# Top-2 dispatch on one core: from every token through every expert to tiles of 256 gathered tokens, with the expert's weights addressed by a register

## The chip, the core and the metric

The kernel runs on one core of one Trainium2 chip. A core has five engines with queues of their own: TensorE (PE in the profile, with its weight loads listed as PEld), VectorE (DVE), ScalarE (ACT), GpSimd (POOL) and SyncE (SP). An engine takes its instructions in order; engines wait for each other, and for DMA transfers, through semaphores. The metric is the time on the device, in microseconds. The kernel before takes 1529.28 us, the median of three runs from 1528.74 to 1529.36 us.

## The reference, cut to what matters

Sixty-four heads of attention with a decay mask give x, and a layer of eight experts follows, of which each token uses its two best.

```python
scores = scale * np.matmul(q, k.transpose(0, 1, 3, 2))       # 8 batches, 8 heads, 576 x 64
ret = scores * Dmat                                          # gamma_h ** (i - j) for i >= j, else 0
x = np.matmul(ret, v)                                        # as (4608 tokens, 512)
noisy_logits = x @ w_gate + np.log1p(np.exp(x @ w_noise)) * noise
top2 = np.argpartition(-noisy_logits, 2, axis=1)[:, :2]      # 2 of 8 experts for each token
top2_w = softmax over the two
for e in range(8):
    for k in range(2):
        mask = top2[:, k] == e
        h = np.maximum(x[mask] @ w1[e], 0.0)                 # 512 -> 1024
        out[mask] += top2_w[mask, k, None] * (h @ w2[e])     # 1024 -> 512
```

## The kernel before

The program is written on a framework that orders the instructions of each engine by their priority and dependences when it is built, and puts in the waits. The order is fixed from then on.

**Attention** (L90 to L157). For each head and each pair of batches GpSimd issues twelve loads that cast to bf16 (L72, L75). TensorE transposes the queries and keys (L85), VectorE copies the result and multiplies it by the decay (L87, L106, L107). Then, for each batch and each block of 128 keys, TensorE makes the scores (L123), ScalarE copies them to SBUF (L126), GpSimd zeroes the part above the diagonal (L128) and TensorE multiplies by the values (L134, L139). ScalarE copies the result out (L153, L154), and SP writes it, transposed, to an HBM buffer xT (L156).

**Router** (L166 to L209). GpSimd reads xT back as bf16 into xTb, 512 tokens at a time (L176). For each of 36 tiles of 128 tokens there are eight matmuls of 8 columns (L183, L186), an exponential and a logarithm on ScalarE with the loads of their tables (L189 to L201), and nine small VectorE instructions that leave the weight of each of the eight experts, zero for six of them, in `gate` (L209).

**Experts** (L211 to L240). For each of the eight experts GpSimd loads the two weight matrices with a cast (L214, L215; two buffers of each). For each of nine groups of 512 tokens TensorE makes the hidden layer: 8 blocks of 128 hidden units with 4 matmuls each, the weights stationary and 512 tokens moving (L222); ScalarE applies the ReLU (L225). Then come 4 tiles of 128 tokens with 8 matmuls each, the hidden layer stationary and 512 columns of w2b moving (L230), and VectorE multiplies by the gate and adds into `out_acc`, which holds the whole output in SBUF (L234, L237). All tokens go through all experts: 8 x 9 x 64 = 4608 matmuls of 512 columns. Finally SP writes out_acc (L243).

## Time and profile before

| | |
|---|---|
| median of the runs | 1529.28 us |
| the profiled execution: span from the first to the last instruction | 1526.2 us |
| HBM read, written | 71.48 MB, 18.87 MB |
| TensorE's mean granted clock | 0.993 |
| matmuls issued: 1568 in attention and router, 4608 in the experts | 6176 |

The page of the profile gives no time of its own beside the span; the median of the runs is 3.1 us longer than the span. The span has three stages that follow each other almost without overlap: attention up to 416.6 us, reading xT back and the router up to about 540 us, and the experts. In the page's line of 40 slices each slice is 38.2 us long. Times of matmuls in the groups are from issue to the modelled end, so that they overlap; the rate is read from the chain of work or from the count in a window.

### The profile page before, as it was taken

How to read it: one execution, taken by the hardware profiler on the slowest of the kernel's cores; microseconds unless marked ns; L12 is line 12 of the kernel's file. 1: busy time of each engine (PE TensorE's matmuls, PEld its weight loads, DVE VectorE, ACT ScalarE, POOL GpSimd, SP SyncE). 2: the span in 40 equal slices, each digit the busy share in tenths (PEclk: the TensorE clock that was granted, in tenths of full speed). 3: DMA queues.
4: the chain of work that ended last, by engine and by line, in shares of the span. 5: the costliest groups of instructions: out<-in, count | busy, mean ns of one | idle time of the engine just before them, and what ended most of it. 6: DMA issues, size and time to landing. Idle time of an engine off the chain costs nothing.

```text
span 1526.2 us, 16572 instructions
## 1 busy us (share of the span) xinstructions
PE 1322.8 (87%) x6081; PEld 590.0 (39%) x6176; DVE 371.8 (24%) x1032; ACT 627.7 (41%) x1275; POOL 412.6 (27%) x738
## 2 busy tenths in 40 slices
PE   5777777777613599999999999999999999999998
PEld 2333333333201244444444444444444444444444
DVE  2222222222123332212221222122212221222122
ACT  4444444444479943333333333333333333333332
POOL 9999999999720000000000000000000000000000
PEclk9999999999999889999999999999999999999999
DMA  6666666665592000120030030020003003000122
GB/s 53 59 58 58 60 59 57 58 60 54 52 190 49 2 1 1 19 37 1 0 56 1 0 56 0 0 47 10 1 4 52 1 0 56 1 0 16 70 81 83
DMA packets 150657, 55.78 MB, mean 37 GB/s; under 512 B 124976, under 2 KB 137776, under 8 KB 150576
## 3 DMA queue, kind: packets, MB, share of 16 engines
q0 software_dynamic: 135088, 35.69, 23.6%
q1 hardware_dynamic: 15488, 19.03, 4.2%
q8 instruction: 48, 0.79, 0.2%
q14 instruction: 33, 0.27, 0.1%
HBM read 71.48 MB, written 18.87 MB: 59 GB/s over the span
## 4 chain that ended last, share of the span: by engine, by line
PE 74%; POOL 14%; ACT 7%; issue 2%; DVE 2%; DMA 0%; ACTq 0%; POOLq 0%
PE po L230 32%; PE phT L222 32%; POOL st L128 4%; PE pv_ps L134 4%; PE st_ps L123 3%; POOL q_bm L72 2%; POOL v_bm L72 2%; ACT L191 2%; PE tr_ps L85 2%; ACT L201 2%; POOL k_bm L72 2%; POOL q_bt L75 2%; POOL v_bt L75 2%; ACT st L126 1%; POOL k_bt L75 1%
## 5 line engine op out<-in xcount | busy, mean ns | idle before, releaser
L225 ACT ACTIVATE hT<-phT 128x512 bf16<-128x512 f32 x576 | 343.6, 597 | 638.1 <-PE phT L222 616.4
L222 PE MATMUL phT<-xTb,w1b 128*128 128x512 bf16 x2256 | 521.2, 384 | 5.1 <-ACT hT L225 2.1
L230 PE MATMUL po<-w2b,hT 128*128 128x512 bf16 x2257 | 511.1, 381 | 2.4
L237 DVE SCALAR_TENSOR_TENSOR out_acc<-po,gate,out_acc 128x512 f32<-128x512 f32 x252 | 189.2, 751 | 683.7 <-PE po L230 652.1
L222 PEld LDWEIGHTS <-w1b 128*128 128x128 bf16 x2304 | 224.8, 98 | 276.7 <-issue 18.4
L230 PEld LDWEIGHTS <-hT 128*128 128x128 bf16 x2304 | 225.6, 98 | 272.1 <-issue 3.6
L214 POOL DMA_DIRECT2D w1b<-in_moe_w_dram x8 | 6.0, 751 | 792.4 <-PE phT L222 789.2
L126 ACT ACTIVATE st<-st_ps 128x512 bf16<-128x512 f32 (+4 forms) x320 | 131.6, 425 | 190.5 <-PE st_ps L144 99.6
L123 PE MATMUL st_ps<-Qs,Ks 64*128 64x512 bf16 (+4 forms) x320 | 130.0, 436 | 46.2 <-DVE Ks L107 35.1
L128 POOL TENSOR_SCALAR_AFFINE_SELECT st<-st 128x512 bf16<-128x512 bf16 (+4 forms) x320 | 147.8, 510 | 19.7 <-ACT st L126 17.6
L134 PE MATMUL pv_ps<-st,v_bm 128*64 128x512 bf16 (+3 forms) x256 | 104.5, 454 | 18.7 <-POOL st L128 18.6
L87 DVE COPY qT<-tr_ps 128x128 bf16<-128x128 bf16 (+1 forms) x160 | 30.3, 215 | 214.1 <-PE tr_ps L85 214.1
L123 PEld LDWEIGHTS <-Ks 64*128 64x128 bf16 (+1 forms) x320 | 32.7, 113 | 115.7 <-issue 65.1
L186 PE MATMUL pn<-wn,xTb 128*128 128x8 bf16 x144 | 9.3, 169 | 53.7 <-ACT ns L189 53.7
L134 PEld LDWEIGHTS <-v_bm 128*64 128x64 bf16 x256 | 38.4, 150 | 40.4 <-issue 19.2
L72 POOL DMA_DIRECT2D q_bm<-in_q_dram x64 | 52.5, 820 | 0.0
L85 PE MATMUL tr_ps<-ident,k_bm 128*128 128x128 bf16 x128 | 25.1, 281 | 30.8 <-DMA k_bm<-in_k_dram 23.1
L72 POOL DMA_DIRECT2D k_bm<-in_k_dram x64 | 51.5, 805 | 0.0
L72 POOL DMA_DIRECT2D v_bm<-in_v_dram x64 | 50.4, 788 | 0.2 <-issue 0.2
L153 ACT ACTIVATE xs<-pv_ps 64x512 f32<-64x512 f32 x64 | 37.6, 587 | 27.3 <-ACT st L126 15.1
L234 DVE TENSOR_SCALAR out_acc<-po,gate 128x512 f32<-128x512 f32 x36 | 27.0, 750 | 83.5 <-PE po L230 83.5
L87 DVE COPY kT<-tr_ps 128x128 bf16<-128x128 bf16 (+1 forms) x160 | 29.0, 214 | 73.7 <-PE tr_ps L85 73.7
(55 smaller groups left out, 630.4 us busy)
## 6 DMA issues: line engine op xcount, KB each, us to landing
xT<-xs SPq DMA_DIRECT2D x64, 144.0 KB, 2.4
out_dram<-out_acc SPq DMA_DIRECT2D x36, 256.0 KB, 2.0
w1b<-in_moe_w_dram POOLq DMA_DIRECT2D x8, 1024.0 KB, 8.8
w2b<-in_moe_w_dram POOLq DMA_DIRECT2D x8, 1024.0 KB, 9.2
xTb<-xT POOLq DMA_DIRECT2D x9, 512.0 KB, 12.6
q_bm<-in_q_dram POOLq DMA_DIRECT2D x64, 64.0 KB, 2.6
k_bm<-in_k_dram POOLq DMA_DIRECT2D x64, 64.0 KB, 2.6
v_bm<-in_v_dram POOLq DMA_DIRECT2D x64, 64.0 KB, 2.7
```

What stands on the lines that cost most here:

```text
L72: nc.gpsimd.dma_start(out=bmain[:, :, bi * D:(bi + 1) * D], in_=src[:STS * P].rearrange("(t p) d -> p t d", p=P))
L75: nc.gpsimd.dma_start(out=btail[:, bi * D:(bi + 1) * D], in_=src[STS * P:])
L85: nc.tensor.matmul(pst[:, :kn], lhsT=src[:kn], rhs=ident[:kn, :kn], is_transpose=True, start=True, stop=True)
L87: nc.vector.tensor_copy(dst[:, j * P:j * P + kn], pst[:, :kn])
L123: nc.tensor.matmul(pst[:kn, :qlen], lhsT=Ksl[:, ko:ko + kn], rhs=Qsl[:, ko:ko + qlen], start=True, stop=True)
L126: nc.scalar.activation(st[:kn, :qlen], pst[:kn, :qlen], Act.Copy, scale=scale)
L128: nc.gpsimd.affine_select(st[:kn, :qlen], st[:kn, :qlen], pattern=[[1, qlen]], base=0, channel_multiplier=-1, compare_op=Alu.is_ge, fill=0.0)
L134: nc.tensor.matmul(po0[:, ko:ko + bn0], lhsT=vj, rhs=st[:kn, 0:bn0], start=(jb == 0), stop=(jb == STS - 1))
L222: nc.tensor.matmul(phT, lhsT=w1b[:, di, fi * P:(fi + 1) * P], rhs=xg[:, di, :], start=(di == 0), stop=(di == KD - 1))
L225: nc.scalar.activation(hT[:, fi, :], phT, Act.Relu)
L230: nc.tensor.matmul(po, lhsT=hT[:, fi, tsub * P:(tsub + 1) * P], rhs=w2b[:, fi, :], start=(fi == 0), stop=(fi == KF - 1))
L237: nc.vector.scalar_tensor_tensor(out_acc[:, t, :], in0=po, scalar=gate[:, t, e:e + 1], in1=out_acc[:, t, :], op0=Alu.mult, op1=Alu.add)
```

## The change

The router's result is used to send each token only to its two experts. The kernel has three functions now.

`attention` is as before, except that ScalarE writes its result as bf16 straight into an SBUF tile xT (L139, L140), and nothing is written to HBM and read back. Two of its pools have one buffer less: the raw inputs two instead of three, the decay vectors one instead of two. Its instructions have other line numbers: the loads L58 and L61, the transposes L71, the scores L109, the selects L114.

`dispatch` makes, for all 4608 tokens at once, the logits (L159), the best two experts (L178 to L199), and for each of the 9216 (token, expert) pairs a slot number in a list sorted by expert, by matmuls with a triangle of ones (L207, L209). Row numbers of tokens are put in the order of the slots by 72 rounds: for each column of 128 tokens and each of their two experts VectorE builds one-hot matrices of 384 and twice 128 columns (L269, L271, L273), and TensorE multiplies them (L277). Beside this each tile of 128 tokens is transposed back (L257), copied by ScalarE (L259), given four columns of its own (two weights, an expert, a slot; L260) and written as one row of 1040 bytes for each token to an HBM buffer xd (L261). Each expert's slots are filled up to a multiple of 256; the number of tiles of 256 slots is fixed at 43, the most that can be needed. `keep` holds for each tile its expert times 4096 (`eoff`) and the tokens' row numbers (`toki`).

`experts` goes through the 43 tiles. GpSimd gathers the tile's rows by two indirect DMAs of 128 rows (L353). TensorE transposes them (L384), loads the tile's offset into a register (L390) and makes the hidden layer with 32 matmuls of 256 columns whose stationary operand is addressed by the register (L399), and the output with 16 matmuls of 512 columns whose moving operand is (L414). The first step of tile i+1 is woven with the second of tile i, two to one. ScalarE and VectorE share the ReLU (L404, L406). ScalarE writes each tile's weighted output to y, which SP writes to an HBM buffer yd (L433, L434); a token's second visit gathers the row of its first (L426), VectorE adds it (L436), and an indirect DMA writes the sum to the token's row of the output (L438). Rows that are not wanted have a number out of bounds and are skipped. The weights of all eight experts, W1 and W2, are loaded once by 16 DMAs (L524, L527) and stay in SBUF.

```diff
+def dispatch(tc, K, xT, wgn, moe_noise, xd, keep):
...
+        for c in range(C):
+            pt = ps.tile([P, DM], BF16, name="pt", bufs=2)
             for di in range(KD):
+                nc.tensor.transpose(pt[:, di * P:(di + 1) * P], xT[:, di, c * P:(c + 1) * P], K["ident"])
+            xr = sp2.tile([P, XW // 2], F32, name="xr")
+            nc.scalar.activation(xr[:, :DM // 2].bitcast(BF16), pt, Act.Copy)
+            V.tensor_copy(xr[:, DM // 2:], pl[:, c, :])
+            nc.sync.dma_start(out=xd[c * P:(c + 1) * P, :], in_=xr)
...
+        for c in range(C):
+            for j in range(2):
+                ohi = sp2.tile([P, 3 * P], BF16, name="ohi")
+                V.tensor_scalar(ohi, K["iota"], hi[:, j, c:c + 1], None, Alu.is_equal)
+                olo = sp2.tile([P, 2, P], BF16, name="olo")
+                V.tensor_scalar(olo[:, 0, :], K["iota"][:, :P], lo[:, j, c:c + 1], K["pidx"][:, 0:1],
+                                Alu.is_equal, Alu.mult)
+                V.tensor_scalar(olo[:, 1, :], K["iota"][:, :P], lo[:, j, c:c + 1], float(c + 1),
+                                Alu.is_equal, Alu.mult)
...
+def experts(tc, K, W1, W2, keep, xd, yd, out):
...
+        def g1(i):
+            r = nc.tensor.value_load(keep["eoff"][0:1, i:i + 1], min_val=0, max_val=(E - 1) * KD * F)
...
+            for fp in range(KF // 2):
+                p1 = ps.tile([P, 2, TS], F32, name="p1", bufs=3)
+                for f2 in range(2):
+                    for di in range(KD):
+                        nc.tensor.matmul(p1[:, f2, :],
+                                         lhsT=W1[:, bass.ds(r + (di * F + (2 * fp + f2) * P), P)],
+                                         rhs=xgT[:, di, :], start=(di == 0), stop=(di == KD - 1))
+                        yield
...
+        def g2(i):
...
+            for fi in range(KF):
+                for s in range(2):
+                    nc.tensor.matmul(po[s], lhsT=hT[:, fi, s * P:(s + 1) * P],
+                                     rhs=W2[:, bass.ds(r + fi * DM, DM)],
+                                     start=(fi == 0), stop=(fi == KF - 1))
...
+            for s in range(2):
+                if i:
+                    nc.gpsimd.indirect_dma_start(
+                        out=pv[:, s, :], out_offset=None, in_=yd[:i * TS, :],
+                        in_offset=IOff(ap=st[i]["pi"][:, s:s + 1], axis=0),
+                        bounds_check=i * TS - 1, oob_is_err=False)
...
         for e in range(E):
-            w1b = wep.tile([P, KD, F], BF16)
-            w2b = wep.tile([P, KF, DD], BF16)
-            for g in range(NGRP):
...
-                for fi in range(KF):
-                    phT = mps.tile([P, GRP], F32, bufs=2)
...
-                        nc.tensor.matmul(phT, lhsT=w1b[:, di, fi * P:(fi + 1) * P],
...
-                        nc.tensor.matmul(po, lhsT=hT[:, fi, tsub * P:(tsub + 1) * P],
```

How the order moves, at the places of which the prediction speaks. First **TensorE in the middle of the experts**; phT and p are the hidden layer's PSUM tiles, W_65 and W_66 the two resident weight tiles, and an ISA row is an instruction of TensorE's sequencer that works out an address from the register. Before:

```order
L222 LDWEIGHTS w1b
L222 MATMUL phT<-xTb,w1b 128x512
L222 LDWEIGHTS w1b
L222 MATMUL phT<-xTb,w1b 128x512
L222 LDWEIGHTS w1b
```

The changed kernel, in the middle of a tile:

```order
L414 LDWEIGHTS hT
L414 ISA
L414 MATMUL po<-W_66,hT 128x512
L399 ISA
L399 LDWEIGHTS W_65
L399 ISA
L399 MATMUL p_10924<-xgT,W_65 128x256
L399 ISA
L399 LDWEIGHTS W_65
L399 ISA
L399 MATMUL p_10924<-xgT,W_65 128x256
```

Each matmul of 256 columns has become four instructions, two of them address arithmetic, and each matmul of 512 columns three. In the program each ISA row holds two or three arithmetic steps on registers: the offset in bytes is the register times two, to which a constant is added.

Second, **GpSimd in the experts**. Before, it only issues the weights of the experts to come:

```order
L214 DMA w1b<-in_moe_w_dram 128x4x1024
L215 DMA w2b<-in_moe_w_dram 128x8x512
L214 DMA w1b<-in_moe_w_dram 128x4x1024
L215 DMA w2b<-in_moe_w_dram 128x8x512
L214 DMA w1b<-in_moe_w_dram 128x4x1024
```

The changed kernel, one tile with its waits (DMASW is GpSimd's own DMAs, DMAHW those of SP; prv is the gathered row of the first visit, xg the gathered tile):

```order
L438 DMA out_dram<-o,oi 4608x512 [waits DMASW6_49,DMASW2_49,DVE_49]
L426 DMA prv_5846<-yd,pi 128x512 [waits DMAHW3_49,DMASW7_49]
L438 DMA out_dram<-o,oi 4608x512 [waits DMASW6_49,DVE_49]
L426 DMA prv_5846<-yd,pi 128x512 [waits DMASW1_49]
L353 DMA xg_5843<-xd,toki 128x260 [waits DVE_49,PE_49]
L353 DMA xg_5843<-xd,toki 128x260 [waits DMASW3_49,PE_49]
```

Six indirect DMAs belong to each tile. The two that write the output wait for VectorE, the first that reads yd waits for SP's write of the tile before, and the two that gather a tile wait for TensorE to have transposed an earlier one. The tile gathered here is seven ahead of the one whose old rows are gathered beside it.

Third, **VectorE in the dispatch**. Before, at the place of the router (nl, ev, msk, gv, gsum and gate are tiles of 8 columns or 1):

```order
L196 TENSOR_TENSOR nl<-nl,pg 128x8
L209 TENSOR_SCALAR gate<-gv,gsum 128x8
L198 MAX mx<-nl 128x8
L195 TENSOR_TENSOR nl<-ns,noise_t 128x8
L190 TENSOR_SCALAR ns<-ns 128x8
```

The changed kernel, in the middle of the 72 rounds (ohi and olo are the one-hot matrices):

```order
L269 TENSOR_SCALAR ohi<-iota_f,hi 128x384
L260 COPY xr<-pl 128x4
L271 TENSOR_SCALAR olo<-iota_f,lo,pidx 128x128
L273 TENSOR_SCALAR olo<-iota_f,lo 128x128
L260 COPY xr<-pl 128x4
L269 TENSOR_SCALAR ohi<-iota_f,hi 128x384
L271 TENSOR_SCALAR olo<-iota_f,lo,pidx 128x128
L273 TENSOR_SCALAR olo<-iota_f,lo 128x128
```

Nine small instructions for each of 36 tiles have gone, and three long ones for each of 72 rounds have come, with the 36 copies into the rows of xd between them.

More of the change, by code (lines that the diff above doesn't have):

```diff
@@ L11 @@
 BF16 = mybir.dt.bfloat16
+I32 = mybir.dt.int32
 AX = mybir.AxisListType.X
@@ L14, with attention @@
 Act = mybir.ActivationFunctionType
-@with_exitstack
-def kernel(
-    ctx: ExitStack,
-    tc: tile.TileContext,
-    q: bass.AP,
-    k: bass.AP,
-    v: bass.AP,
-    moe_w_gate: bass.AP,
-    moe_w_noise: bass.AP,
-    moe_noise: bass.AP,
-    moe_w1: bass.AP,
-    moe_w2: bass.AP,
-    out: bass.AP,
-):
+P = 128
+N = 4608
+NCOL = N // P
+E = 8
+F = 1024
+DM = 512
+KD = DM // P
+KF = F // P
+TS = 256
+NTILE = 43
+HPE = N // P
+NHI = E * HPE
+XW = DM + 8
+BIG = 1.0e6
+IOff = bass.IndirectOffsetOnAxis
+def attention(tc, q, k, v, xT):
     nc = tc.nc
     B, H, S, D = q.shape
-    N, DD = out.shape
-    E = moe_w_gate.shape[1]
-    F = moe_w1.shape[2]
-    assert (B, H, S, D) == (8, 8, 576, 64)
-    assert (N, DD, E, F) == (4608, 512, 8, 1024)
-    P = 128
-    NT = N // P
-    KD = DD // P
-    KF = F // P
-    GRP = 512
-    NGRP = N // GRP
     STS = 4
     STL = S - STS * P
-    dram = ctx.enter_context(tc.tile_pool(name="dram", bufs=1, space=bass.MemoryType.DRAM))
-    xT = dram.tile([P, KD, N], F32)
     scale = 1.0 / math.sqrt(D)
     with tc.tile_pool(name="attn_const", bufs=1) as consts, \
-         tc.tile_pool(name="attn_head", bufs=2) as headp, \
-         tc.tile_pool(name="attn_raw", bufs=3) as rawp, \
+         tc.tile_pool(name="attn_head", bufs=1) as headp, \
+         tc.tile_pool(name="attn_raw", bufs=2) as rawp, \
          tc.tile_pool(name="attn_qk", bufs=2) as qkp, \
          tc.tile_pool(name="attn_st", bufs=4) as stp, \
-         tc.tile_pool(name="attn_psum", bufs=2, space=bass.MemoryType.PSUM) as ps, \
-         tc.tile_pool(name="attn_out", bufs=3) as outp:
+         tc.tile_pool(name="attn_psum", bufs=2, space=bass.MemoryType.PSUM) as ps:
         ident = consts.tile([P, P], BF16)
```

400 lines of the change are left out of this document (324 added, 76 removed).

## The prediction

> **What bounds the kernel now.** I read the page first: its busy times and its line of 40 slices.
>
> ```profile
> span 1526.2 us, 16572 instructions
> ...
> PE 1322.8 (87%) x6081; PEld 590.0 (39%) x6176; DVE 371.8 (24%) x1032; ACT 627.7 (41%) x1275; POOL 412.6 (27%) x738
> ...
> PE   5777777777613599999999999999999999999998
> ```
>
> The slices show two kernels in one: up to slice 15 TensorE has gaps, from slice 16 on it is full. The shares over the whole span hide that, so I cut it at the ends of the stages (columns: length, busy time and count of each engine, granted clock, DMA share, GB/s).
>
> ```profile
> core 0: us, PE busy (x) PEld busy (x) DVE busy (x) ACT busy (x) POOL busy (x), PEclk, DMA share, GB/s
> 0.00:416.60 416.60, 302.92 (x1280) 126.54 (x1280) 116.93 (x384) 186.83 (x529) 391.47 (x711) 1.00 0.63 57
> 416.60:540.00 123.40, 42.20 (x359) 20.55 (x365) 38.96 (x353) 103.99 (x181) 11.35 (x15) 0.93 0.48 76
> 540.00:1523.00 983.00, 977.73 (x4444) 442.94 (x4532) 215.63 (x297) 336.92 (x565) 9.82 (x12) 1.00 0.11 23
> ```
>
> GpSimd bounds attention (391 of 417 us). The middle stage is mostly ScalarE (104 of 123 us). The experts are TensorE alone, at the full clock, and how fast is read from the chain in order of time:
>
> ```profile
> 552.67 6.91 PE phT L222 x32
> ...
> 587.29 6.91 PE po L230 x32
> ```
>
> 32 matmuls of 512 columns take 6.91 us: 0.216 us each, 0.42 ns per column. 4608 of them would be 995 us; some run before 540 us. This stage is 64% of the span, and three quarters of its work is multiplied by a gate of zero.
>
> **The change part by part.** I build the changed kernel's span stage by stage.
>
> *Attention* keeps its GpSimd instructions in the same order, with the first two weight loads pushed in near its end. With one raw buffer less, a pair's inputs are overwritten two pairs later; a pair takes 416.6/32 = 13.0 us, and its inputs are read within that. That cover hides the edit; without it each pair would wait about one landing (2.6 us, row below), 83 us in all. I take 416.6, with ScalarE's xT write in the place of the old one.
>
> *Dispatch* is a chain on VectorE, whose instructions I price by these rows (group: count, busy us, mean ns; two rows of the timeline: start, duration):
>
> ```profile
> L234 DVE TENSOR_SCALAR out_acc<-po,gate 128x512 f32<-128x512 f32 x36 | 27.0, 750 | 83.5 <-PE po L230 83.5
> L209 DVE TENSOR_SCALAR gate<-gv,gsum 128x8 f32<-128x8 f32 x36 | 8.1, 225 | 0.0
> L190 DVE TENSOR_SCALAR ns<-ns 128x8 f32<-128x8 f32 x36 | 5.8, 161 | 32.6 <-ACT ns L189 32.6
> L191 ACT ACT_TABLE_LOAD x31 | 39.8, 1283 | 0.5
> ...
> 433.01 0.23 DVE L200 TENSOR_SCALAR ev<-nl,mx 128x8 f32<-128x8 f32 x1
> ...
> 433.14 0.23 DVE L203 TENSOR_SCALAR msk<-nl,mx 128x8 f32<-128x8 f32 x1
> ```
>
> A VectorE instruction with a scalar from memory costs 0.225 us for 8 columns and 0.750 for 512, so 1.04 ns per column on top of about 0.22; with a constant the fixed part is 0.16. Independent ones start 0.13 us apart though they last 0.23, so 0.1 of the fixed part overlaps. One round of the 72 is then 0.62 + 0.35 + 0.35 - 0.27 = 1.05 us, together 76 us. The bounds: 53 us if SBUF operands stream at twice the rate (the 750 ns row reads PSUM), 95 us with no overlap. I take 76, since every row measured has the overlap, and 4 us for the 36 copies between. Around them: logits and their copy 6 us (288 short matmuls at most), two tables and two activations 3.5, fifteen instructions of 288 columns at 0.46 and eleven small ones 9, 36 dependent additions at 0.2 7, ranks 4, tail 5. Dispatch: 76 + 4 + 34.5 = 114.5 us, against 123.4 for the stage that it replaces. It ends at 531.
>
> Three things lie beside it. ScalarE's 36 copies of a token tile, at the 0.6 us that it needs for 512 columns (row below), are 22 us. The writes to xd hold up VectorE's copies only if four of them need longer than eight rounds (8.4 us). And the weights:
>
> ```profile
> L126 ACT ACTIVATE st<-st_ps 128x512 bf16<-128x512 f32 x64 | 38.2, 597 | 134.0 <-PE st_ps L144 99.6 <-PE pv_ps L139 22.7 <-PE st_ps L123 10.3
> ...
> 432.00:436.00 4.00, 0.60 (x12) 0.48 (x12) 0.67 (x5) 3.55 (x6) 1.22 (x2) 1.00 1.31 206
> ...
> q_bm<-in_q_dram POOLq DMA_DIRECT2D x64, 64.0 KB, 2.6
> out_dram<-out_acc SPq DMA_DIRECT2D x36, 256.0 KB, 2.0
> ```
>
> While weights and xTb load together the queues move 206 GB/s. Sixteen weights of 1.05 MB and the 4.8 MB of xd are 21.6 MB, 105 us: all has landed near 522. That is 9 us ahead of need, the thinnest cover in the plan.
>
> *Start of the experts*: two indirect issues at the 0.82 us of a GpSimd DMA, a landing of 2.6, transposes, and ScalarE's copy of 1024 columns (1.1): 6 us, so 537. *End*: two VectorE additions, two issues, a landing, the closing: 6 us.
>
> *A tile* decides. TensorE's streaming is 32 x 256 + 16 x 512 + 8 x 128 columns at 0.42 ns: 7.35 us. That alone would be 316 us for 43 tiles. But each tile now passes 80 address computations (ISA) through TensorE's sequencer, 32 weight loads and 48 matmuls that take their address from a register, and 32 plain instructions. Nothing in this trace computes an address on TensorE. The nearest rows are instructions that the sequencers handle themselves (min/median/max ns), and the router's short matmuls:
>
> ```profile
> L85 PEldq EVENT_SEMAPHORE  x128: 51/51/51, 6.0 to 406.4; - x128
> ...
> L258 POOLq MOVE  x1: 35/35/35, 0.1 to 0.1; - x1
> ...
> L258 ACTq EVENT_SEMAPHORE  x1: 17/17/17, 0.7 to 0.7; - x1
> ...
> 471.68 0.25 PE L186 MATMUL pn<-wn,xTb 128*128 128x8 bf16 x4 [5.80 <-ACT ns L189]
> ...
> L186 PE MATMUL pn<-wn,xTb x144: 165/168/215, 426.4 to 525.4; 128*128 128x8 bf16 x144
> ```
>
> Four pairs of weight load and matmul take 0.25 us, of which the last takes 0.168: a pair each 27 ns, 13.5 ns for a plain instruction. TensorE's own sequencer instruction, a semaphore wait, takes 51 ns, and a register move (GpSimd's) 35. So an ISA costs between 51 ns (the arithmetic free) and 51 + 3 x 35 = 156; I take the middle, 104. An instruction with a register address costs between 13.5 and 51 + 35 = 86; I take 51, the row of the same sequencer. Then 80 x 0.104 + 80 x 0.051 = 12.4 us, the plain ones 0.4, and 1.4 for the register load (between the 51 ns of a sequencer instruction and the 2.0 us of a DMA's landing) and the waits. **A tile takes 14.2 us**, and streaming hides beneath it: TensorE is bound by its sequencer. The bounds are 7.35 (80 x 0.0645 = 5.2 would vanish under streaming) and 80 x 0.242 + 2.8 = 22.2 us.
>
> [...]
>
> GpSimd's six DMAs per tile come next (group rows as above):
>
> ```profile
> L72 POOL DMA_DIRECT2D q_bm<-in_q_dram x64 | 52.5, 820 | 0.0
> L75 POOL DMA_DIRECT2D v_bt<-in_v_dram x64 | 36.1, 564 | 0.9 <-issue 0.9
> L215 POOL DMA_DIRECT2D w2b<-in_moe_w_dram x8 | 7.1, 885 | 41.3 <-PE po L230 30.8 <-PE phT L222 6.9 <-DMA xTb<-xT 3.6
> ```
>
> An issue costs 0.56 to 0.89 us; reading 128 row numbers may double it. Six are 3.4 to 10.7 us, and the second output write waits out the first's landing (2.0 less an issue). At 0.82 that is 6.1 us: hidden under 14.2. The first gather from yd waits for ScalarE's two copies (1.2) and SP's write (2.0 to 2.6) after the tile's last matmul, some 4.5 us, with the output writes and gathers of later tiles behind it on GpSimd; with five issues after it, it is through at 8.6, inside a tile of 14.2. Should the tile shrink below that, this wait is the next thing late. VectorE (two additions 1.5, two ReLUs 1.2, eleven small ones 2) and ScalarE (1.1 + 1.2 + 1.2) are under 5 us.
>
> **The sum.** 416.6 + 114.5 + 6 + 43 x 14.2 + 6 = 1154 us of span. The median of the runs lies 3.1 us above the profiled span, so **1157 us**.
>
> **The rivals.** *A: register addresses are nearly free.* Then streaming, or GpSimd at up to 10 us, bounds the tile: 7.35 to 10 us, 546 + 43 x 8.5 = 912 us, up to 976. For it speaks how close plain instructions follow each other; against it that TensorE's only sequencer instruction in the trace takes 51 ns where ScalarE's, the same, takes 17 (rows above). *B: slower.* If an instruction with a register address is not sent until the matmul ahead of it is done, nothing overlaps on TensorE any more. A matmul of 512 columns takes 379 ns from issue to end (row below), one of 256 about 275, a weight load 98. 32 x (0.208 + 0.098 + 0.275) + 16 x (0.104 + 0.098 + 0.379) = 28 us, and 546 + 43 x 28 = 1750 us. It decides from 22.9 us on: (1529.3 - 546)/43.
>
> ```profile
> L230 PEld LDWEIGHTS <-hT 128*128 128x128 bf16 x2304 | 225.6, 98 | 272.1 <-issue 3.6
> L222 PE MATMUL phT<-xTb,w1b x2256: 375/379/635, 482.8 to 1515.2; 128*128 128x512 bf16 x188
> ```
>
> For B speaks that no such instruction is in the trace, against it that streams of matmuls with waits overlap freely here.
>
> [...]
>
> *C: a late dispatch*: the weights or xd's writes starve the rounds (95 us for the rounds, 30 more for the writes): 1200 us. *D: it does not skip what it says*: 43 tiles run whether filled or not, 11008 slots for 9216 pairs; this is in the sum already and has no chance of its own.
>
> **How the numbers follow.** The forecast, a sequencer-bound tile of 10 to 20 us, has 0.65, with C inside it; A has 0.23, B 0.09, and 0.03 are left for tiles of 20 to 22.9 us. The forecast alone spans 976 to 1406. The range for eight in ten takes in most of A and stops where the upper bounds meet: 915 to 1400 us. A measurement of this kernel tells 0.2% from no change. Only B is slower: slower 0.09, faster 0.90, the same 0.01.
>
> **What would show it.** In the changed profile: the middle slices of TensorE well under nine tenths in the experts though nothing releases it late (idle before L399 put down to issue); 43 tiles evenly 14 us apart; ISA rows near 104 ns on TensorE's sequencer; GpSimd idle in each tile. A: TensorE at nine tenths, or GpSimd full, and tiles of 7 to 10 us. B: matmuls that start only at the end of the one before. Dispatch is right if L353's first start is near 531 us. The forecast is wrong if the tile is not bound by TensorE's sequencer.

## The result, and the profile after

The changed kernel takes 1022.4 us (median of four runs, 1019.43 to 1022.85), the kernel before 1529.0 us beside it (1528.37 to 1529.36). The ratio is 0.668, with a 95% interval of 0.667 to 0.669. The forecast was 1157 us: right in sign, inside its range, and 135 us too long. The profiled run took 1022.85 us, its span 1021.1 us. Of the kernels below, two have one execution that is over 1.5% longer than the fastest of its kernel (1033.6 us with the weights in the attention, 1100.4 us with six buffers), and their medians are given without it.

First the view of the changed kernel cut at the ends of its stages (columns as before: length, busy time and count of each engine, granted clock, DMA share, GB/s).

```profile
core 0: us, PE busy (x) PEld busy (x) DVE busy (x) ACT busy (x) POOL busy (x), PEclk, DMA share, GB/s
0.00:418.20 418.20, 303.01 (x1280) 126.08 (x1281) 120.56 (x387) 189.41 (x529) 396.60 (x724) 1.00 0.57 38
418.20:560.40 142.20, 58.84 (x513) 39.76 (x512) 86.54 (x365) 24.70 (x41) 15.18 (x20) 0.90 0.77 144
560.40:1001.50 441.10, 412.68 (x2408) 219.51 (x2408) 173.87 (x600) 149.02 (x214) 254.03 (x251) 0.98 0.38 120
1001.50:1021.10 19.60, 0.11 (x1) 0.00 (x0) 1.50 (x2) 1.04 (x2) 5.05 (x5) 0.50 0.17 54
```

Set against the terms of the sum (the first tile's matmuls start at 567.7 us, so 7.3 us of the third row are the start of the experts):

| Term | Predicted | Measured | Difference |
|---|---|---|---|
| Attention | 416.6 | 418.2 | +1.6 |
| Dispatch | 114.5 | 142.2 | +27.7 |
| Start of the experts | 6 | 7.3 | +1.3 |
| 43 tiles | 43 x 14.2 = 610.6 | 433.8 = 43 x 10.09 | -176.8 |
| End | 6 | 19.6 | +13.6 |
| Span | 1153.7 | 1021.1 | -132.6 |

So the tile decided, as the prediction said, and it came out 29% shorter. Two terms were too small. The rows on TensorE's sequencer (PEldq is what the sequencer does in the queue of weight loads; count: min/median/max ns, first and last start):

```profile
L399 PEldq FUSED_REGOPS  x2752: 37/46/51, 567.3 to 992.7; - x197
...
L414 PEldq FUSED_REGOPS  x688: 42/46/51, 574.6 to 1000.0; - x172
...
L390 PEldq TENSOR_LOAD <-eoff x14: 295/299/494, 555.9 to 566.1; - x14
...
L390 PEldq TENSOR_LOAD <-eoff x29: 297/300/451, 694.1 to 983.2; - x29
```

An address computation, which the order listed as ISA, is the row FUSED_REGOPS: two or three operations in one instruction, 46 ns where the prediction took 104 and set the floor at 51. The register load is 300 ns. The last two rows are of two windows: fourteen loads run before the first tile, twenty-nine later, one per tile.

The pace shows in the starts of the output's matmuls (L414), eight of them in 3.9 us:

```profile
L414 PE MATMUL po<-W,hT x8: 376/376/377, 744.8 to 748.7; 128*128 x8
```

Two matmuls of W1 and one of W2 form a group. A group takes 3.9/7 = 0.56 us here and 0.545 us in the median of the starts from 590 to 690 us, while its 1024 columns stream in 0.43. The group holds five address computations, five instructions with a register address and one plain weight load: if the sequencer works them off one after the other, (545 - 5 x 46 - 13.5)/5 = 60 ns are left for an instruction with a register address, where the prediction took 51. This is an estimate from these rows and from the prediction's 13.5 ns.

From the starts of every 32nd matmul at L399 a tile takes 8.9 to 9.2 us from the third to the thirteenth, 9.5 to 9.9 from the fourteenth to the twenty-second, mostly 10.0 to 10.6 after that, and 11.7 to 12.3 in the last three. What the other engines waited for in this time (engine, line, releaser: us in total, times, longest):

```profile
DVE oi L365 <- DMA out_dram<-o,oi: 115.3, 39, 5.5
DVE pi L375 <- DMA prv<-yd,pi: 64.0, 25, 4.4
PEld L399 <- issue: 55.6, 184, 2.4
...
DVE isA L359 <- DMA xg<-xd,toki: 49.5, 26, 5.2
```

VectorE stands for transfers that still read its small buffers (L365, L375), or have yet to fill a gathered tile (L359), and ReLUs and additions stand behind it. In the last tiles, where no gathers of xd are left, GpSimd shows a chain that repeats every 12 us: an output write, the wait for its landing, the second one, two gathers, their landing, VectorE's addition. VectorE's waits for the small buffers stand in the same chain, just ahead of the addition (two timelines, GpSimd and VectorE: start, duration, [idle before, releaser]).

```profile
954.51 1.01 POOL L438 DMA_INDIRECT out_dram<-o,oi  x1 [4.31 <-DVE o L436]
958.06 1.00 POOL L438 DMA_INDIRECT out_dram<-o,oi  x1 [2.55 <-issue]
959.36 1.04 POOL L426 DMA_INDIRECT prv<-yd,pi  x1 [0.30 <-issue]
960.71 1.02 POOL L426 DMA_INDIRECT prv<-yd,pi  x1 [0.30 <-issue]
966.61 1.01 POOL L438 DMA_INDIRECT out_dram<-o,oi  x1 [4.88 <-DVE o L436]
...
960.91 0.16 DVE L365 SCALAR_TENSOR_TENSOR oi<-isA,tokf 128x2 int32<-128x2 f32 x1 [4.24 <-DMA out_dram<-o,oi]
965.51 0.16 DVE L375 SCALAR_TENSOR_TENSOR pi<-isA,pf 128x2 int32<-128x2 f32 x1 [4.43 <-DMA prv<-yd,pi]
965.58 0.74 DVE L436 SCALAR_TENSOR_TENSOR o<-po,g,prv 128x512 f32<-128x512 f32 x1
```

In the dispatch one wait stands out, and a smaller one behind it:

```profile
DVE nl L165 <- DMA noise<-in_moe_noise_dram: 30.6, 1, 30.6
DVE xr L260 <- DMA xd<-xr: 16.1, 14, 3.5
```

The noise is issued at 417.75 us, when its buffer opens, and lands at 454.1, behind the weights. VectorE does nothing for 30.6 us of that time.

### The profile page after: what moved, and what is told of

Same layout as the page of the kernel before. It is cut to its first block, busy times and chain, and to the rows that moved or that the text cites. A ratio compares the mean times of both kernels' runs of the same rounds, so it can differ in the third digit from the quotient of the medians.

```text
span 1021.1 us, 16704 instructions
## 1 busy us (share of the span) xinstructions
PE 774.6 (76%) x4201; PEld 385.3 (38%) x4201; DVE 382.5 (37%) x1354; ACT 364.2 (36%) x785; POOL 670.9 (66%) x998
## 5 line engine op out<-in xcount | busy, mean ns | idle before, releaser
L399 PE MATMUL p<-xgT,W 128*128 128x256 bf16 x1376 | 325.0, 273 | 19.0 <-DVE hT L406 14.0
L414 PE MATMUL po<-W,hT 128*128 x688 | 259.7, 381 | 4.1 <-DVE hT L406 4.0
L399 PEld LDWEIGHTS <-W 128*128 x1376 | 132.6, 96 | 192.2 <-issue 55.6
L438 POOL DMA_INDIRECT out_dram<-o,oi x86 | 86.9, 1011 | 119.8 <-DVE o L436 52.1
L109 PE MATMUL st_ps<-Qs,Ks 64*128 64x512 bf16 (+4 forms) x320 | 129.7, 435 | 46.7 <-DVE Ks L93 35.1
L114 POOL TENSOR_SCALAR_AFFINE_SELECT st<-st 128x512 bf16<-128x512 bf16 (+4 forms) x320 | 148.1, 514 | 18.2 <-ACT st L112 16.6
L353 POOL DMA_INDIRECT xg<-xd,toki x86 | 86.4, 1005 | 84.6 <-DVE toki L330 39.6
L404 ACT ACTIVATE hT<-p 128x512 bf16<-128x512 f32 x86 | 51.4, 597 | 239.2 <-PE p L399 231.5
L426 POOL DMA_INDIRECT prv<-yd,pi x84 | 85.8, 1021 | 28.1 <-issue 25.7
L436 DVE SCALAR_TENSOR_TENSOR o<-po,g,prv 128x512 f32<-128x512 f32 x86 | 64.2, 746 | 37.8 <-DMA prv<-yd,pi 24.2
L109 PEld LDWEIGHTS <-Ks 64*128 64x128 bf16 (+1 forms) x320 | 32.6, 113 | 117.2 <-issue 67.2
L414 PEld LDWEIGHTS <-hT 128*128 128x128 bf16 x688 | 66.4, 97 | 21.2 <-DVE hT L406 4.4
L433 ACT ACTIVATE y<-po,g 128x512 f32<-128x512 f32 x86 | 54.8, 685 | 41.2 <-PE po L414 33.5
L386 ACT ACTIVATE xgT<-pt 128x1024 bf16<-128x1024 bf16 x43 | 44.0, 1024 | 55.2 <-DVE cm L370 48.4
L277 PE MATMUL pT<-olo,ohi 128*128 128x256 bf16 x216 | 42.6, 308 | 23.3 <-DVE olo L273 18.4
L406 DVE TENSOR_SCALAR hT<-p 128x512 bf16<-128x512 f32 x86 | 58.7, 682 | 0.0
L58 POOL DMA_DIRECT2D q_bm<-in_q_dram x64 | 52.6, 822 | 0.1
```

The source lines that it names most:

```text
L109: nc.tensor.matmul(pst[:kn, :qlen], lhsT=Ksl[:, ko:ko + kn], rhs=Qsl[:, ko:ko + qlen], start=True, stop=True)
L114: nc.gpsimd.affine_select(st[:kn, :qlen], st[:kn, :qlen], pattern=[[1, qlen]], base=0, channel_multiplier=-1, compare_op=Alu.is_ge, fill=0.0)
L353: nc.gpsimd.indirect_dma_start(out=xg[:, s, :], out_offset=None, in_=xd[:, :], in_offset=IOff(ap=keep["toki"][:, 2 * i + s:2 * i + s + 1], ...
L399: nc.tensor.matmul(p1[:, f2, :], lhsT=W1[:, bass.ds(r + (di * F + (2 * fp + f2) * P), P)], rhs=xgT[:, di, :], start=(di == 0), stop=(di == ...
L406: V.tensor_relu(hT[:, 2 * fp:2 * fp + 2, :], p1)
L414: nc.tensor.matmul(po[s], lhsT=hT[:, fi, s * P:(s + 1) * P], rhs=W2[:, bass.ds(r + fi * DM, DM)], start=(fi == 0), stop=(fi == KF - 1))
```

## The experiments

Two theories stood against each other. **S**: TensorE's sequencer sets the tile. **G**: GpSimd's and VectorE's order of transfers, landings and dependent work sets it, and the sequencer has room. For the dispatch: **N**, the wait for the noise is all on the path, against **W**, the weights' transfers hold the rest as well.

The kernel before takes 1529.0 to 1529.2 us whenever it runs. The changed kernel doesn't: 1022.4 us in its first runs, 1061.5 in its last (below). The experiments were made on three chips, and only on the last of them beside the changed kernel. So times are compared where they were made together, and where a stage is set against the first runs of the changed kernel, the text says so. On one chip the fixed experts, the twelve small buffers, the early noise and the longer arithmetic were run; on a second the pinned order with and without registers, the weights in the attention, and all of these; on the third six buffers with and without registers, the changed kernel again and the twelve small buffers again.

### Fixed experts

```diff
-  lhsT=W1[:, bass.ds(r + (di * F + (2 * fp + f2) * P), P)],
+  lhsT=W1[:, (i * E // NTILE) * KD * F + di * F + (2 * fp + f2) * P: ... + P],
```

and the same at W2.

> Left out of the computation: the choice of the expert. Each tile takes the weights of a fixed expert (the constant i*8//43), so the register arithmetic and the register-addressed loads and matmuls of the tiles are gone; tables, gathers, scatters and every other instruction stay. Theory S (TensorE's sequencer sets the tile: a group of two W1 matmuls and one W2 matmul takes 0.545 us for 0.43 us of streaming): the group falls to 0.43 us and the tile from 10.08 us to what comes next, GpSimd's six indirect transfers at 1.31 us from start to start, 7.9 us, with some waits 8.2; 43 x 1.9 = 81 us less, 941 us (920 to 965). Rival G (the tile is set by GpSimd's order of scatter, landing and gather, about 10 us, and the sequencer has room): the tile stays at 9.7 to 10.1 us, 1005 to 1022 us.

Measured: 1022.1 us (1018.9 to 1023.5). The time of theory S (941 us) didn't come, although the group fell to the 0.43 us that it had named. Theory G's time came (1005 to 1022 us), its even tiles of 9.7 to 10.1 us only in the mean. Four starts in 1.3 us:

```profile
L414 PE MATMUL po<-W,hT x4: 379/379/379, 820.3 to 821.6; 128*128 128x512 bf16 x4
```

The tiles became uneven, from 7.4 us, which is the streaming bound of the prediction (7.35), to 15 us, 9.97 on average. TensorE now stood for a ReLU of VectorE:

```profile
PE p L399 <- DVE hT L406: 63.2, 28, 4.2
```

where the changed kernel had 14.0 us in 19 waits. This run also shows what came after one such stop (timeline, and the same stretch in windows):

```profile
824.61 0.38 PE L399 MATMUL p<-xgT,W 128*128 128x256 bf16 x2 [2.65 <-DVE hT L406]
...
826.10 0.63 PE L399 MATMUL p<-xgT,W 128*128 128x256 bf16 x2
...
826.10:829.00 2.90, 2.90 (x12) 1.65 (x11) 1.06 (x4) 0.65 (x2) 1.50 (x3) 0.50 0.29 91
829.40:833.00 3.60, 3.60 (x32) 2.59 (x31) 0.84 (x3) 2.43 (x4) 2.59 (x3) 1.00 0.70 237
```

After 2.65 us without work the matmuls go on at the full rate for about a microsecond and then at a granted clock of 0.50 until 829. The length of the one stop does not decide it: in the changed kernel (the profile with the span of 1021.1 us) stops of 2.16 us (up to 954.88) and 2.09 us (up to 978.96) are followed within 0.2 us by a clock of 0.50, for 3.3 us each, while after a stop of 2.15 us (up to 966.98) it stays at 1.00 for 11.5 us. What brings it down no run here shows.

What follows: there is a second limit close behind the sequencer, near 10 us a tile on average, and TensorE meets it waiting for VectorE. How much the arithmetic costs, the time doesn't tell, since the changed kernel was not run on this chip. The one unedited experts' stage here is that of the early noise (below), 478.7 us from the first gather to the end against 456.6 with fixed experts, and in 24 us of it lie the long rows of which the last experiment speaks. In the first runs of the changed kernel it took 460.7.

### Longer register arithmetic

```diff
-  W1 = wp.tile([P, E * KD * F], BF16, name="W1")
+  W1 = wp.tile([P, 2 * E * KD * F], mybir.dt.uint8, name="W1")
...
-  lhsT=W1[:, bass.ds(r + (di * F + (2 * fp + f2) * P), P)],
+  lhsT=W1[:, bass.ds(r + 2 * (di * F + (2 * fp + f2) * P), 2 * P)].bitcast(BF16),
```

and the same at W2, with the register in bytes.

> The resident weights are declared as bytes and viewed as bf16, with the register in bytes: the same number of register-arithmetic instructions at L399 and L414, but each with one more member, a division by two (46 ns is the row with three members, 37 ns the shortest, with two); nothing is left out. Eighty of them run in a tile. Theory S: whatever the row grows by is paid in full: 43 x 80 ns = 3.44 us of time for each ns; 9 ns more would make 1053 us, 40 ns more 1160 us, and the group of 0.545 us grows by five times the row's growth. Rival G (sequencer not the bound up to 10 us a tile): the first 11 ns (0.9 us a tile) are free, and beyond that half or less of the growth shows in early tiles: 1022 us at 9 ns, 1120 us or less at 40 ns.

Measured: 1142.4 us (1141.5 to 1143.9). The row grew from 46 to 85 ns, 39 ns. The starts:

```profile
L414 PE MATMUL po<-W,hT x6: 376/377/377, 744.9 to 748.6; 128*128 x6
...
L414 PEldq FUSED_REGOPS  x5: 85/85/85, 745.5 to 748.5; - x5
```

In the median a group takes 0.742 us, 197 ns more, for 5 x 39 = 195. So the growth of the sequencer's work is paid in full. Tiles take 12.1 to 12.3 us up to the thirteenth and 12.8 to 13.1 after it, evenly to the last. Theory S gave 1022 + 3.44 x 39 = 1156 us, theory G at most 1120. The 14 us under S lie in the late tiles: against the first runs of the changed kernel, tiles 3 to 22 grow by 3.1 to 3.3 us (80 x 39 ns are 3.1), those after them by 2.7 in the mean, the last three by 0.6 to 1.2. There the changed kernel loses time to waits, which a longer tile covers.

Both limits are thus real. At 46 ns the sequencer sets the tile up to about the twenty-second, at 9.1 us and, with the register load in the stream, at 9.5 to 9.9. After that the waits add to it, and with a longer row the sequencer alone sets the tile.

The step at the fourteenth tile is in this kernel too, 0.7 us, and it falls where the register loads change: fourteen are done before the first tile, from 694.1 us on each stands in the tile's own stream. Its rows (300 ns, and 151 and 18 ns for the bounds check) account for 0.47 us of the 0.7; the rest has no row.

### Twelve small buffers

```diff
-  tc.tile_pool(name="moe_s", bufs=4) as sm, \
+  tc.tile_pool(name="moe_s", bufs=12) as sm, \
```

> The small per-tile tables of VectorE (oi, pi, g and their like) get 12 buffers in place of 4, nothing else; GpSimd's and TensorE's orders stay as they are. Theory V (the 0.9 us by which the average tile is over the sequencer's 9.1 to 9.2 us comes from VectorE standing at L365 and L375 until an earlier scatter or gather that reads the old buffer has landed, with relus queued behind): these waits are gone, the tiles from 600 to 930 us go at 9.2 us as the first ten did, and 30 to 40 us go: 985 us (978 to 996). Rival G (GpSimd's chain of scatter, its landing, gather, its landing and L436 closes over 10 us by itself): L365 and L375 wait no more, L436 waits in their place, and under 12 us go: 1010 to 1022 us.

> The kernel with twelve small buffers once more. If the long rows belong to the program: about 50 of them again and 1038 to 1050 us. If to the chip or the run: none, and the time without their 32 us, 1011 us (1005 to 1018), which would be the gain of 10 us that rival G gave the longer buffers.

Measured: 1043.3 us (1038.3 to 1050.6) and, with the changed kernel beside it, 1053.3 (1049.7 to 1061.6) against 1061.5 (1056.6 to 1063.4): ratios to the kernel before of 0.688 [0.687, 0.689] and 0.693 [0.691, 0.695]. The 30 to 40 us of theory V didn't come: the gain is 8 us where the two ran together, under 12 as G had it, with 42 us of long rows (below) in the one profile and 30 in the other. The waits at L365 and L375 are gone, and others have their place, now ahead of the ReLUs:

```profile
DVE isA L359 <- DMA xg<-xd,toki: 108.8, 38, 5.3
DVE o L436 <- ACT y L433: 102.3, 30, 4.8
DVE o L436 <- DMA prv<-yd,pi: 34.6, 22, 5.2
```

VectorE takes up the small tables as soon as a buffer is free, and then waits for their gather. What is gained lies in the last tiles: in both runs the last four take 9.7 to 9.9 us, where the last three of the changed kernel take 11.7 to 12.3 in its first runs and 9.3 to 13.0 beside the twelve buffers. So the chain of 12 us hung on the small buffers, and without it the tile is back at the sequencer's pace with its register load. Theory V left that load out of its 9.2 us. The second part of the expectation, the long rows, is taken up below.

### The early noise

```diff
-  noise = sp.tile([P, C, E], F32)
-  nc.sync.dma_start(out=noise, in_=moe_noise.rearrange("(c p) e -> p c e", p=P))
+  noise = K["noise"]        # loaded ahead of the attention into the constants' pool
```

> The noise is loaded at the start of the kernel into a buffer that is never reused, in place of after the attention behind the weights' transfers. Theory N (the 30.6 us in which VectorE stood at L165 for it are all on the path to the first gather): first gather at 530 to 533 us in place of 560.4, time 992 to 996 us. Rival W (the weights and the xd writes still share the transfers until about 517 us, and the xd rows and their writes, which took half of VectorE's time at 480 to 500 us, hold the one-hot rounds): VectorE starts 30 us earlier and then waits for the row copies; first gather at 543 to 555 us, time 1005 to 1017 us.

Measured: 1034.6 us (1029.2 to 1037.9), with no changed kernel beside it. So the time decides nothing here, but the rows of the dispatch do: the first gather starts at 548.8 us in place of 560.4. That is 11.6 of the 30.6 us. Most of the rest went where W said:

```profile
DVE xr L259 <- DMA xd<-xr: 30.5, 30, 3.2
```

against 16.1 us in the changed kernel: the row copies wait for writes to xd that share the transfers with the weights, which go on until about 500 us in both. Theory N is refuted: the wait for the noise hid another behind it.

### The weights in the attention

```diff
-  attention(tc, q, k, v, xT)
-  for e in range(E):
-      nc.gpsimd.dma_start(out=W1[...], in_=moe_w1[e]...)   # and W2
+  attention(tc, q, k, v, xT, load_expert)   # load_expert(h) in the second pair of head h
```

with the early noise.

> The noise is loaded at the start, and the sixteen weight transfers are issued two at a time in the second pair of each head of the attention in place of after it; nothing else moves. Theory W (what held the dispatch after the noise came early was the weights' transfers, behind which the xd rows and so the one-hot rounds stood): VectorE works from 423 us without the 30.6 and the 16.1 us: first gather at 514 us counted from an attention end of 418; GpSimd, 95% busy in the attention, issues the sixteen at 0.8 to 0.9 us, so the attention ends 13 us later, at 432 us, first gather at 527 us (515 to 535); time 985 us if the tiles stay as in the changed kernel, 1000 us if they go as in the run with the noise alone. Rival A (the weights' traffic holds the attention's own loads): the attention ends 30 us or more late and nothing is gained on the run with the noise alone, first gather at 545 us or later.

Measured: 1023.6 us (1014.9 to 1025.4). Rival A: the attention ends at 469.5 us, 51 us late, and the first gather is at 567.9. The profile is of the execution of 1033.6 us, but the kernel with all of it (below) has the same edit, and its first gather is at 567.8 us, in an execution within 0.1% of its others. The end of the attention and the dispatch by themselves, and what TensorE waited for in the attention:

```profile
418.20:469.50 51.30, 33.49 (x142) 14.27 (x142) 10.43 (x37) 20.34 (x58) 39.47 (x73) 1.00 0.63 62
469.50:567.90 98.40, 53.32 (x513) 36.34 (x512) 85.42 (x365) 24.31 (x41) 4.70 (x7) 0.96 0.15 50
...
PE tr_ps L71 <- DMA q_bm<-in_q_dram: 69.2, 16, 9.0
```

Theory W was right for its own stage: free of the weights, the dispatch takes 98.4 us in place of 142.2, with VectorE busy for 85. But the weights cost the attention what they save here: TensorE waits 16 times for the attention's own loads of q, where it waits once in the changed kernel, for 9.0 us.

### The pinned order

```diff
+  def pin(ins):          # each GpSimd transfer of the stage behind the one before it
...
+  pin(... prv gathers of tile i + 1, both halves)
   o(i)
+  pin(... output write of tile i, half 0); pin(... xd gathers of tile i + 4); pin(... output write, half 1)
...
+  tc.keep_in_program_order(V.tensor_scalar(isA, ...))    # the tables of tile i + 2
```

> Only the order of the experts' stage is changed: GpSimd's queue is pinned to, per tile, the two yd gathers of the next tile, scatter, the two xd gathers of the tile four on, scatter; VectorE's small tables of a tile are pinned to two tiles ahead of its use, when its gather has long landed. Every instruction is as before, the buffers too. Theory Q (what the tiles take over the sequencer's own time is VectorE and GpSimd standing in order behind landings): tiles of 9.1 us while the registers are loaded ahead (the first 14), 9.85 us after that (the register load of 0.3 + 0.15 us and its company in TensorE's queue, as in the step from 9.0 to 9.85 us at the 14th tile of the changed kernel), last matmul at 567 + 13 x 9.1 + 30 x 9.85 = 981 us and a tail of 14 to 20 us: time 1000 us (990 to 1008). Rival C (the scatters' landings and the yd round trip close a chain of 10 us per tile in any order): 1015 us or more, tiles of 10 us from the first on.

> The pinned order and the fixed experts together (left out: the choice of the expert, as before). Theory Q with S as the second limit: with the landings out of the way the sequencer is the bound, so that without its arithmetic the tile falls to GpSimd's six transfers of 1.31 us, 7.9 us, or a little more: 567 + 43 x 8.0 = 911 us and a tail of 16: time 930 us (915 to 955), 70 us under the pinned kernel with registers, where the same edit alone gave nothing. Rival C: tiles of 10 us again, 1005 us or more, no difference between the two pinned kernels.

Measured: 1071.5 us (1065.2 to 1077.5) with registers, 1051.4 (1048.7 to 1051.8) with fixed experts. The order made it worse, by a wait that I had not foreseen: on this chip the experts take 509.8 us from the first gather to the end, against 464.0 in their own order, with the weights in the attention. TensorE stands for the gathers of xd, and GpSimd for SP's write:

```profile
PE pt L396 <- DMA xg<-xd,toki: 51.3, 41, 5.9
...
POOL prv L444 <- DMA yd<-y: 151.8, 39, 17.2
```

Behind the gathers of yd, which wait for that write, those of xd are issued too late for the transposes two tiles on, and every other tile takes 12 us. This is not rival C either, whose chain should have held every tile at 10. The pair does tell one thing: with the same order and on the same chip, and with no long rows in either, the arithmetic is worth 20 us, while the late gathers hold both kernels (51 and 100 us at the transposes), where 43 tiles x 16 groups x 0.11 us would be 76.

### All of it, and six buffers

```diff
+  rs[:] = nc.values_load_multi_w_load_instructions(keep["eoff"][0:1, i:min(i + 4, NTILE)], ...)   # every fourth tile
-  r = nc.tensor.value_load(keep["eoff"][0:1, i:i + 1], min_val=0, max_val=(E - 1) * KD * F)
...
-  NX = 4
+  NX = 6                    # in the second pair only, with the gathers six tiles ahead and the weights after the attention
```

> The pinned order, the early noise and the weights in the attention together, and the register loads four tiles at a time without the bounds check (11 loads of four registers in place of 43 loads, 43 checks). Theory Q, S and W add up: first gather at 527 us, tiles of 9.1 to 9.2 us throughout, 534 + 43 x 9.15 = 927 us, tail 16: time 946 us (930 to 962). If the register load is not what makes the step at the 14th tile, tiles of 9.8 us from then on: 968 us. If the chain of landings (rival C) holds: 980 us or more.

> The pinned order again, now with six xg buffers in place of four and each tile's xd gathers issued six tiles ahead (in the pinned kernel TensorE stood at the transposes L396 for gathers that were issued too late), the early noise, and the register loads four tiles at a time without the bounds check. Theory Q with S: nothing stands behind a landing any more and the sequencer sets the tile, 9.1 to 9.2 us from the first to the last: first gather 549 us, 556 + 43 x 9.15 = 950 us, tail 15 us, time 968 us (955 to 985), faster than both kernels. If the register load is not what makes the step at the 14th tile: 9.85 us from there on, 988 us. Rival C (the yd round trip and the two scatters one behind the other make 10 us or more in any order): 1000 us or more.

> The same with fixed experts (left out: the choice of the expert). Theory Q with S: with nothing else in the way the register arithmetic now costs what it takes over the next bound, which is GpSimd's six transfers at 1.31 us (7.9 us) or the matmuls' own 7.4 us: tile 8.0 us, 556 + 344 = 900 us, tail 15 us: time 918 us (905 to 940), 50 us under the kernel with registers. Rival C: no difference between the two, 1000 us or more.

Measured: 1058.9 us (1058.6 to 1059.3) for all with four buffers; there the late gathers are back (49.6 us at the transposes, 36 times), so it decides nothing on the sum. Tiles between two such waits take 8.5 to 8.7 us late in the stage, where the shortest late tile of the pinned kernel on the same chip takes 9.8: with the register loads four at a time and no check the step is gone. With six buffers 1076.8 us (1074.2 to 1087.8), and 1033.2 (1030.0 to 1039.8) with fixed experts, beside 1061.5 for the changed kernel. TensorE no longer waits for gathers, but for its own sequencer:

```profile
PE p L416 <- issue: 62.2, 105, 1.3
...
L416 PEldq FUSED_REGOPS  x2752: 2/46/1237, 557.0 to 1048.6; - x197
```

Of this run's address computations 102 take over 0.4 us, 70 us in all, and most of TensorE's idle time put to issue in the two layers (57 of 74 us) has one of them in it. The expectation of 968 us failed by 109. The two kernels differ by 44 us, but that is not the price of the arithmetic: the one has these long rows, and the other stops too, with 53 us of TensorE's idle time put to issue in the experts. With registers, none of these versions is shown to beat the changed kernel: six buffers take 15 us more beside it, and no changed kernel ran beside the other. No run here shows the 9.1 us held through the whole stage.

### The changed kernel again

> The changed kernel itself, unedited, on the chip of this call. It tells whether the register-arithmetic rows of 0.6 to 0.7 us in place of 46 ns, of which the run with twelve small buffers had 53 and the run with the early noise 41, and the changed kernel none, belong to the program or to the chip and the run. If to the program: none here, 1022 us. If to the chip: some here as well, 1025 to 1055 us, or none in any run of this call.

Measured: 1061.5 us (1056.6 to 1063.4) on this chip, 39 us over the first runs. The row behind it:

```profile
L399 PEldq FUSED_REGOPS  x2752: 2/46/1190, 568.4 to 1033.2; - x197
...
L414 PEldq FUSED_REGOPS  x688: 2/46/863, 582.4 to 1040.5; - x172
```

The median is 46 ns as before, but the longest is 1.19 us where it was 51 ns. 46 of these rows are over 0.4 us, 30 us in all; in the first runs' profile, and in every one made beside the pinned order, none is. With twelve buffers there were 53 and 64, with the early noise 41, with six buffers 102 (70 us), with the longer arithmetic 2. So they come and go with the same program unedited, and belong to the chip or to the run, which these runs don't tell apart. On the same two chips TensorE also stops in the kernels with fixed experts, which have no address computation: 10 and 53 us of its idle time in the experts are put to issue, against 4 beside the pinned order. So it is not the arithmetic alone that stalls. What causes it stays open.

## Why the prediction was right, and where not

**Attention** came within 1.6 us, and its covers held.

**Dispatch** was 27.7 us short, and not by its working. The rounds, taken at 1.05 us, took 0.80 (75 instructions in the 20 us from 520 to 540, three to a round), near the lower bound of 53 us for all: the 384 columns of L269, which it reads from SBUF, take 421 ns in the median, by an estimate 0.52 ns each on top of the prediction's 0.22 us, where it had 1.04 each; alone, the stage takes 98.4 us, 16 under the forecast. The step "all has landed near 522" held: the last weights land at 502 us, the last write to xd at 519.5. What the prediction had not asked is what waits behind the weights in the transfers until then. The noise did, a load of 0.15 MB without a term in the sum (30.6 us), and the writes to xd, of which the prediction had said that they hold up VectorE only if four need longer than 8.4 us (16.1 us, with a median landing of 3.8). Rival C named this, "the weights or xd's writes starve the rounds", and put it at 95 + 30 us.

**The tile** was 4.1 us too long, and the term is the address computation: 80 x (104 - 46) = 4.6 us. The other terms moved little: the register address 60 in place of 51 (+0.7), and the register load and the waits 1.2 in place of 1.4. The mechanism was right as far as it went. TensorE's sequencer does set the group (the longer arithmetic), and with its register loads it sets the tiles up to about the twenty-second; by the prediction's own sum with 46 and 60 ns, 80 x 0.106 + 0.4 = 8.9 us, measured 8.9 to 9.2. The floor of 51 ns was wrong in kind: the semaphore wait of 51 ns was no lower bound for the instructions that compute, with a median of 46 ns and a shortest of 37.

Over the whole stage the forecast is right in the main, and not in full. It said that it would be wrong if the tile were not bound by the sequencer. At the sequencer's pace 13 tiles of 9.1 and 30 of 9.8 would be 412 of the 434 us (an estimate from the rows above), and waits make the rest. But another limit stands close: fixed experts take the arithmetic away, and in the one pair without long rows, which late gathers hold, 20 us come of it, not 76. What bounds beside it is not quite the wait that the prediction had named for a smaller tile ("Should the tile shrink below that, this wait is the next thing late"), the first gather from yd behind SP's write. In the changed kernel GpSimd waits for that write 5.8 us in all; it becomes late, with 151.8 us, only where the order is pinned. What waits is VectorE, 115.3 us for the landings of the output writes and 64.0 for those of the gathers from yd, with ReLUs and additions behind it, and GpSimd 49.9 us for the additions. The prediction gave VectorE under 5 us of work a tile and no wait. GpSimd's six transfers were priced at 0.82 us and may double; an indirect one takes 1.0 us and starts 1.31 after the one before, 7.9 us for six.

**Rivals.** A was close in its number (7.35 to 10 us a tile, up to 976 us) and wrong in its reason, since register addresses aren't free. B is refuted: matmuls go on while the sequencer computes, a group of three in 0.545 us where B had 28/16 = 1.75.

**The end** took 19.6 us and not 6. The prediction counted two issues and a landing. In order there are a gather from yd, its landing, the addition, an output write, its landing, the second write, its landing and the closing:

```profile
1003.73 1.04 POOL L426 DMA_INDIRECT prv<-yd,pi  x1 [0.30 <-issue]
1005.07 1.01 POOL L426 DMA_INDIRECT prv<-yd,pi  x1 [0.30 <-issue]
1008.34 1.01 POOL L438 DMA_INDIRECT out_dram<-o,oi  x1 [2.26 <-DVE o L436]
1011.27 0.99 POOL L438 DMA_INDIRECT out_dram<-o,oi  x1 [1.92 <-DMA out_dram<-o,oi]
```

The terms' errors of +1.6, +27.7, +1.3, -176.8 and +13.6 us made -132.6. The time lies in the range because the tile's bounds were kept open downwards to pure streaming; that the dispatch and the end missed the other way brought it 41 us nearer to the forecast, and that is luck.

## What to carry to other kernels

When one limit is lifted, price the next one with its waits and not with its busy time alone: GpSimd was busy for 58% of the experts' stage and VectorE for 39%, and yet their order of issue, landing and work after it made a chain of 12 us in the last tiles. A load that nobody waits for before may be the first thing late behind a new bulk transfer, as here the noise (0.15 MB, 30.6 us); list every transfer that is issued after it, however small. And before calling a run the effect of an edit, run the unedited kernel beside it: this one differs by 4% between two sets of runs, while the medians of the kernel before agree within 0.1%.

## What the runs showed of the hardware that I had not expected

- Register arithmetic on TensorE's sequencer took a median of 46 ns (37 to 51) for two or three operations in one instruction, and 85 ns with a division as one more. The 39 ns of growth were paid in full: five of them are 195 ns, and the group grew by 197, from 0.545 to 0.742 us, with 0.43 us of streaming.
- An instruction of TensorE with a register address took about 60 ns of its sequencer, against 13.5 for a plain one. Both are estimates: (545 - 5 x 46 - 13.5)/5 from the group of the changed kernel, (742 - 5 x 85 - 13.5)/5 = 61 from the one with the longer arithmetic, and half of the prediction's 27 ns a pair, (250 - 168)/3, from the router's short matmuls in the kernel before.
- On two of three chips, single address computations took 0.4 to 1.4 us in place of the median of 46 ns (85 in the sixth), 41 to 102 times in five runs and twice in a sixth; on the third chip, and in the first runs of the changed kernel, none did. The kernel before did not show it in its time.
- Stops of 2.09 and 2.16 us in the changed kernel and of 2.65 us with fixed experts were followed by half of TensorE's granted clock for about three microseconds, the first two within 0.2 us after work began again, the third after about a microsecond; another stop of 2.15 us in the changed kernel was not.
- Sixteen transfers of weights, 17 MB, lengthened the attention by 51 us although without them the transfers had been busy for only 57% of its time.
